# A softmax-attention and gated-FFN kernel on one core: down weights split one tile later, the last direct scores after the last product, two units in other blocks

## The chip, the cores and the metric

The kernel runs on one core of a Trainium2 chip. The metric is device time in microseconds (us). TensorE (PE) multiplies, VectorE (DVE) and ScalarE (ACT) work on tiles in SBUF and PSUM, GpSimd (POOL) does a little elementwise work and issues some DMAs, SyncE (SP) issues most DMAs. Each engine works through its own list of instructions in the order in which the program wrote them down, and semaphores hold it back where it needs another's result.

## The reference: what is computed

```python
xn = _layernorm(x)                         # x: 1 x 2048 x 512
s  = attention(xn, wqkv, wo)               # 32 heads of 16, softmax over all 2048 keys
g  = _silu((_silu(xn @ w_gate) * (xn @ w_up)) @ w_down)      # F = 1792
return x + s * g
```

Attention is `softmax(q k^T / 4) v` per head, then a product with `wo`. Everything is float32.

## The kernel before, in words

A prologue (about 165 us) normalises x, transposes it and makes q, k and v, which go to memory in DRAM. Then one main loop does attention and the FFN side by side on TensorE, and after it a short tail finishes the output.

**Attention in units and blocks.** A unit is one group of 4 heads (8 groups, `NG`) with 512 queries (4 of them, `NB`): 32 units, u0 to u31. Each goes over 16 key tiles of 128 keys. A unit is cut into blocks of 3 to 6 key tiles, by the planner at L460 to L478: units in `FINE` in four blocks of 4, unit 28 (`units - 4`) as 6, 6, 4, unit 0 as 4, 6, 6, unit 31 as 4, 3, 3, 3, 3, all others as two blocks of 5 and one of 6, the 6 where the FFN tile beside it is the largest. There are 101 blocks, numbered 0 to 100 in order of time.

**One block** is one call of `run(u, first, n)` (L856). It first does the scores of its n key tiles, mixed with products of the FFN, and then all its values (L916, `values`, matmul at L376: eight matmuls to a key tile). Each key tile has two score pairs (j = 0, 1), and each pair two halves. A pair takes one of two ways:
- *direct* (event `D`): two score matmuls at L872 into one of two double banks `score[0]`, `score[1]` in turn, then the exponential on ScalarE from there (L888, `pr<-score`). A direct score must wait until ScalarE is done with the score two before it.
- *copied* (events `A` and `B`): one matmul for each half into the one spare bank (`acc`), each moved out by VectorE (L900 and L906, `pr<-acc`), and at the end of the block one exponential in place (L912, `pr<-pr`). `B` must wait for the copy of `A`, the next `A` for the copy of `B`.

An `F` event is one step of the FFN: a pair of matmuls (`bankx`, `banky`, L186), taken from a generator by `fill` (L439). One FFN tile goes with one block.

**The order of events** is written by `events(n, f)` (L480) for n key tiles and f FFN steps: two direct scores at the start, the others spread with a gap of 4 to 5 places, the copies between them. In the list that it returns, the last event is always a product. `run` walks through the list.

**FFN tiles** come from `ffn(b)` (L195), b being 512 tokens. The 14 tiles of F are two groups of 7. For each group there are first seven *gate tiles* (gate and up products, f = 24 steps), each followed by tanh on ScalarE (L217) and two VectorE instructions (L218, L219) that give the hidden tile, and then four *down tiles* (21 steps each), evacuated by VectorE (L238 and L239, or L242 and L243 in the second group). After the last group of the last b comes a projection of the output for other tokens (`project_out`, two tiles of 9 steps and twelve of 12). With the second group's down tiles, `after` holds further work: `store_gate` (L188) and, for the last b, `next_out` (L261), which splits attention outputs and output weights for the projection.

**Splits.** A float32 operand is used as a high and a low part, so each gate-weight tile (`split_gu`, L130: three instructions), each hidden tile (`split_hidden`, L171: two) and each down-weight tile (`split_wd`, L151: a cast into `wd[:, f, 0]` and a subtraction into `wd[:, f, 1]`) is split on VectorE. These instructions are not written at once: they go into a list, `chores`, with a cost in steps. `run` takes chores from it (L908) when they fit in ahead of the next copy by its own reckoning, or freely when no copy is left; `tidy()` (L139) without an argument writes all of them at once. At the last event of a block (`final`, L876) and behind the block's events (L913) `tidy()` is called. `finish(u)` (L404) puts the closing work of a unit into the same list at the second direct score of the next unit: a transpose (L387), a reciprocal (L392), a scaling (L396) and, for every second group of heads, another transpose (L412).

**Loads.** `load_gu` (L121) and `load_wd` (L146) issue DMAs on SyncE. The raw down weights have one buffer (`wdr`), the raw gate weights two (`gur`). In `ffn`, a gate tile i loads the down weights of tile i and queues the gate split of tile i + 1 and the gate loads of tile i + 2 at its first step; the down-weight split of tile i is queued two steps before its end, so that it is written at the end of the same block.

Of the kernel before, what the change touches and what calls it, by code (L numbers as in the profile page):

```python
# [41 lines left out]
EARLY = 2  # L42
PROBS = 12
EPS = 1e-5
FINE = (27, 29, 30, 31)
QSLOT = (0, 1, 0)
KSLOT = (0, 0, 1)

# [2 lines left out]
def tile_block(ctx: ExitStack, tc: tile.TileContext, x, wqkv, wo, w_gate, w_up, w_down, out):  # L51
# [94 lines left out]
    def load_wd(i):  # L146
        raw = one.tile([P, D], F32, tag="wdr", name="wdr")
        sp.dma_start(raw, w_down[(i % NF) * P:(i % NF + 1) * P])
        wdr[i] = raw
# [45 lines left out]
    def ffn(b):  # L195
        for grp, part in enumerate(GROUPS):
            nf = part.stop - part.start
            for f in range(nf):
                i = b * NF + part.start + f
                if i:  # L200
                    load_wd(i)
                if i + 1 < NB * NF:
                    split_gu(i + 1)
                if i + 2 < NB * NF:
                    load_gu(i + 2)
                hi, lo = gu.pop(i)
                n = 0
                for c in range(DC):
                    for wt, j in ((hi, 0), (hi, 1), (lo, 0)):
                        both(wt[:, c], fx[:, j, c], n == 0, n == 3 * DC - 1)  # L210
                        n += 1
                        if n == 3 * DC - 2 and now > 0:
                            split_wd(f, i)
                        if n == 3 * DC:
                            th = one.tile([P, TB], F32, tag="th", name="th")
                            ga = two.tile([P, TB], F32, tag="ga", name="ga")
                            act(th, bankx, AF.Tanh, scale=0.5)  # L217
                            dve.scalar_tensor_tensor(ga, th, 1.0, bankx, op0=ALU.add, op1=ALU.mult)  # L218
                            dve.scalar_tensor_tensor(ga, ga, 0.5, banky, op0=ALU.mult, op1=ALU.mult)  # L219
                            kept.append((f, ga))  # L220
                            if now == 0:
                                split_wd(f, i)
                            if now >= 0:
                                split_hidden()
                            if grp == 1 and f == nf - 1 and b + 1 < NB:
                                load_fx(b + 1, 0)
                                load_fx(b + 1, 1)
                            elif grp == 1 and f == nf - 1:
                                load_wo(0)
                        yield 3 * DC - n  # L230
            for t in range(NT):
                n = 0
                for f in range(nf):
                    for a, w in ((0, 0), (0, 1), (1, 0)):
                        both(hh[:, f, a, t * P:(t + 1) * P], wd[:, f, w], n == 0, n == 3 * nf - 1)
                        n += 1
                        if n == 3 * nf and grp == 0:
                            dve.tensor_copy(facc[:, t], bankx)  # L238
                            dve.tensor_add(facc[:, t], banky, facc[:, t])  # L239
                        elif n == 3 * nf:  # L240
                            y = two.tile([P, D], F32, tag="ga", name="y")
                            dve.tensor_add(y, bankx, facc[:, t])  # L242
                            dve.tensor_add(y, banky, y)  # L243
                            after.append(partial(store_gate, y, b * TB + t * P))
                            if b == NB - 1:
                                after.append(partial(next_out, t))
                        yield 3 * nf - n
# [4 lines left out]
    def load_wo(c):  # L252
        wor[c] = one.tile([P, D], F32, tag="wdr", name="wor")
        sp.dma_start(wor[c], wo[c * P:(c + 1) * P])
# [206 lines left out]
    for u in range(units):  # L461
        opened.append(len(blocks))
        if u == units - 1:
            ns = [4, 3, 3, 3, 3]
        elif u == 0:
            ns = [4, 6, 6]
        elif u in FINE:
            ns = [4] * 4
        elif u == units - 4:
            ns = [6, 6, 4]  # L470
        else:
            ns = [5] * 3
            far = sizes[len(blocks):len(blocks) + 3]
            ns[far.index(max(far)) if far[1] < max(far) else 1] = 6
        kt = 0
        for n in ns:
            blocks.append((u, kt, n))
            kt += n  # L478

    def events(n, f):  # L480
        length = 2 * n + f
        need = 2 * n - max(2, (10 * length + 46) // 40)
        fit = 1 if ends and length < 24 else (10 * length + 34) // 112
        copied = max(0, min(need, fit)) if now else 0
        direct = 2 * n - copied
        gap = max(4, min(5, (length - 8) / max(1, direct - 2)))
        marks = [(0, "D"), (1, "D")] + [(7 + gap * i, "D") for i in range(direct - 2)]
        marks += [(2.2 + max(5.6, min(8, (length - 5) / (2 * copied))) * i, "AB"[i % 2]) for i in range(2 * copied)]
        marks.sort()
        out = []  # L490
        at = left = 0
        for t, kind in marks:
            while left < f - 1 and at < t:
                out.append((at, "F"))
                left += 1
                at += 1
            out.append((at, kind))
            at += 1 if kind == "D" else 0.5
        return direct, out + [(at + i, "F") for i in range(f - left)]
# [348 lines left out]
    on = [att.tile([P, TB], F32, name=f"on{b}") for b in range(NB)]  # L848

    now = 0  # L850
    split_hidden()
    split_wd(0, 0)
    tidy()
    ends = []

    def run(u, first, n):  # L856
        nonlocal lower
        g, b = divmod(u, NB)
        q = qst[u % 2]
        f = 0 if blocked() or not sizes else sizes.pop(0)  # L860
        direct, todo = events(n, f)
        if now == 0:
            for _ in range(4):
                todo.insert(0, todo.pop(max(i for i, (_, e) in enumerate(todo) if e == "F")))
        pairs = [(kt, j) for kt in range(first, first + n) for j in range(2)]
        straight, copies = pairs[:direct], pairs[direct:]
        probs, waiting = {}, []

        def scores(bank, kt, j, h):
            k, kc = kst[(g * NB + kt // CT) % RING], kt % CT  # L870
            r = slice(h * HALF, h * HALF + NROW)
            mm(bank, k[r, j, kc * P:(kc + 1) * P], q[r, j], start=True, stop=True)  # L872

        done = 0
        copying = [t + 1.5 for t, e in todo if e in "AB"]
        final = len(todo) - 1  # L876
        free = 0
        for at, (t, e) in enumerate(todo):
            if at == final:
                tidy()  # L880
            if e == "F":
                fill(1)
            elif e == "D":
                kt, j = straight[done]
                for h in order():
                    scores(score[done % 2][:, h], kt, j, h)
                probs[kt, j] = ppool.tile([P, 2, TB], F32, tag="pr", name="pr")
                act(probs[kt, j], score[done % 2], AF.Exp, scale=0.25)  # L888
                done += 1
                if done == 2:  # L890
                    while ends:
                        ends.pop(0)()
                    out_steps()
            elif e == "A":
                kt, j = copies.pop(0)
                waiting.append((kt, j))
                scores(spare_bank, kt, j, 0)
                lower = True
                probs[kt, j] = ppool.tile([P, 2, TB], F32, tag="pr", name="pr")
                dve.tensor_copy(probs[kt, j][:, 0], spare_bank)  # L900
                free = copying.pop(0) + 3
            else:
                kt, j = waiting[-1]
                scores(spare_bank, kt, j, 1)
                lower = False
                dve.tensor_copy(probs[kt, j][:, 1], spare_bank)  # L906
                free = copying.pop(0) + 3
            while chores and at < final and (not copying or max(free, t) + chores[0][0] <= copying[0] + 0.5):  # L908
                free = max(free, t) + chores[0][0]
                chores.pop(0)[1]()  # L910
        for kt, j in waiting:
            act(probs[kt, j], probs[kt, j], AF.Exp, scale=0.25)  # L912
        tidy()  # L913
        out_splits()
        catch_up()
        values(u, range(first, first + n), probs)  # L916
# [103 lines left out]
```

## Time and profile before

| | before |
|---|---|
| median of 3 runs | 1423.17 us (1421.42 to 1423.23) |
| the profiled execution | 1421.64 us |
| span of its instructions | 1419.9 us |
| granted TensorE clock | 1.000 |
| DMA moved | 148.17 MB, 104 GB/s on average |

The profile is of one execution; its span runs from the first to the last instruction. A line of a view names the line of the kernel (L376), the engine, the operation and `out<-in` by the names of the tiles. An idle time stands in brackets or behind a bar, with what ended it. The ends of matmuls are modelled, so two matmuls that look back to back can hide a short wait; the distance between starts is the safer reading.

### The profile page before, as it was taken

How to read it: one execution, taken by the hardware profiler on the slowest of the kernel's cores; microseconds unless marked ns; L12 is line 12 of the kernel's file. 1: busy time of each engine (PE TensorE's matmuls, PEld its weight loads, DVE VectorE, ACT ScalarE, POOL GpSimd, SP SyncE). 2: the span in 40 equal slices, each digit the busy share in tenths (PEclk: the TensorE clock that was granted, in tenths of full speed). 3: DMA queues.
4: the chain of work that ended last, by engine and by line, in shares of the span. 5: the costliest groups of instructions: out<-in, count | busy, mean ns of one | idle time of the engine just before them, and what ended most of it. 6: DMA issues, size and time to landing. Idle time of an engine off the chain costs nothing.

```text
span 1419.9 us, 27729 instructions
## 1 busy us (share of the span) xinstructions
PE 1403.0 (99%) x11227; PEld 847.5 (60%) x11227; DVE 756.3 (53%) x1279; ACT 1082.0 (76%) x1235; POOL 92.7 (7%) x104
## 2 busy tenths in 40 slices
PE   9999999999999999999999999999999999999998
PEld 7778665556555655565556555655565555564555
DVE  5543465355546553555455645554555355456556
ACT  5733587788788877787888787878787778687885
POOL 4200200000000000000000000000000000001333
PEclk9999999999999999999999999999999999999999
DMA  6768652043543421154514303365224112233333
GB/s 216 262 246 243 177 122 46 13 96 89 120 106 102 118 56 35 50 124 102 138 56 111 84 12 79 84 147 127 72 70 115 39 37 70 62 114 112 116 95 115
DMA packets 126956, 148.17 MB, mean 104 GB/s; under 512 B 12524, under 2 KB 79340, under 8 KB 126052
## 3 DMA queue, kind: packets, MB, share of 16 engines
q1 hardware_dynamic: 121620, 125.79, 34.7%
q0 software_dynamic: 4912, 20.12, 3.8%
q8 instruction: 91, 1.49, 0.4%
q14 instruction: 45, 0.37, 0.1%
q10 hardware_dynamic: 288, 0.39, 0.1%
HBM read 106.68 MB, written 39.58 MB: 103 GB/s over the span
## 4 chain that ended last, share of the span: by engine, by line
PE 94%; DVE 2%; ACT 2%; DMA 1%; issue 1%; SPq 0%; DVEq 0%; ACTq 0%
PE acc L376 30%; PE bankx L186 23%; PE score L872 16%; PE banky L186 10%; PE ps L626 6%; PE acc L872 3%; PE ps L628 3%; ACT pr L888 1%; DVE pr L900 0%; DMA v_d<-vt 0%; PE acc L601 0%; ACT pr L912 0%; DMA wraw<-in_A_wqkv_dram 0%; PE ps L657 0%; PE acc L957 0%
## 5 line engine op out<-in xcount | busy, mean ns | idle before, releaser
L888 ACT ACTIVATE pr<-score 128x1024 f32<-128x1024 f32 x862 | 812.0, 1033 | 244.5 <-PE score L872 243.2
L376 PE MATMUL acc<-pr,vst 128*17 128x512 f32 x4096 | 461.4, 593 | 0.0
L872 PE MATMUL score<-qst,kst 50*128 50x512 f32 x1724 | 396.1, 417 | 3.2 <-ACT pr L888 3.1
L186 PE MATMUL bankx<-fx,guh 64*128 64x512 f32 x896 | 331.5, 393 | 0.3 <-DVE ga L218 0.2
L186 PE MATMUL banky<-fx,guh 64*128 64x512 f32 x896 | 323.3, 393 | 0.3 <-DVE ga L219 0.3
L376 PEld LDWEIGHTS acc<-pr,vst 128*17 128x17 f32 x4096 | 111.3, 97 | 294.1 <-issue 284.0
L872 PEld LDWEIGHTS score<-qst,kst 50*128 50x128 f32 x1724 | 172.5, 184 | 158.6 <-issue 72.3
L900 DVE COPY pr<-acc 128x512 f32<-128x512 f32 x162 | 112.0, 691 | 171.6 <-PE acc L872 167.0
L186 PE MATMUL bankx<-wd,hh 64*128 64x512 f32 x672 | 200.2, 392 | 0.0
L186 PE MATMUL banky<-wd,hh 64*128 64x512 f32 x672 | 196.6, 391 | 0.0
L186 PEld LDWEIGHTS bankx<-fx,guh 64*128 64x128 f32 x896 | 166.4, 186 | 19.9 <-issue 0.9
L186 PE MATMUL banky<-fx,gul 64*128 64x512 f32 x448 | 175.3, 391 | 0.0
L186 PE MATMUL bankx<-fx,gul 64*128 64x512 f32 x448 | 175.3, 391 | 0.0
L186 PEld LDWEIGHTS banky<-fx,guh 64*128 64x128 f32 x896 | 166.3, 186 | 6.2 <-DVE ga L219 0.6
L912 ACT ACTIVATE pr<-pr 128x1024 f32<-128x1024 f32 x162 | 166.6, 1081 | 0.0
L906 DVE COPY pr<-acc 128x512 f32<-128x512 f32 x162 | 111.9, 691 | 88.4 <-PE acc L872 72.9
L872 PE MATMUL acc<-qst,kst 50*128 50x512 f32 x324 | 130.5, 403 | 5.2 <-issue 2.5
L186 PEld LDWEIGHTS bankx<-wd,hh 64*128 64x128 f32 x672 | 124.8, 186 | 13.1
L218 DVE SCALAR_TENSOR_TENSOR ga<-th,bankx 128x512 f32<-128x512 f32 x56 | 38.5, 687 | 166.3 <-ACT th L217 166.3
L186 PEld LDWEIGHTS banky<-wd,hh 64*128 64x128 f32 x672 | 124.9, 186 | 3.1
L186 PEld LDWEIGHTS bankx<-fx,gul 64*128 64x128 f32 x448 | 83.7, 187 | 9.9
L186 PEld LDWEIGHTS banky<-fx,gul 64*128 64x128 f32 x448 | 83.6, 186 | 2.6
(171 smaller groups left out, 1317.8 us busy)
## 6 DMA issues: line engine op xcount, KB each, us to landing
gur<-in_B_w_gate_dram SPq DMA_DIRECT2D x56, 256.0 KB
gur<-in_B_w_up_dram SPq DMA_DIRECT2D x56, 256.0 KB
wdr<-in_B_w_down_dram SPq DMA_DIRECT2D x56, 256.0 KB
kst<-k_d SPq DMA_DIRECT2D x192, 64.0 KB
qst<-q_d SPq DMA_DIRECT2D x192, 64.0 KB
fx<-xt_d SPq DMA_DIRECT2D x24, 512.0 KB
q_d<-parts SPq DMA_DIRECT2D x16, 512.0 KB
k_d<-parts SPq DMA_DIRECT2D x16, 512.0 KB
```

The source lines that it names most:

```text
L186: mm(banks[i], lhs[halves[i]], rhs[halves[i]], start=start, stop=stop)
L218: dve.scalar_tensor_tensor(ga, th, 1.0, bankx, op0=ALU.add, op1=ALU.mult)
L376: mm(acc[0][h * 32:h * 32 + DH + 1], v[:, kt % CT, h * (DH + 1):(h + 1) * (DH + 1)], probs[kt, h // 2][:, h % 2], start=kt == 0, stop=kt = ...
L626: mm(ps, w, a[:, c], start=n == 0, stop=n == 3 * DT - 1)
L628: mm(ps, a[:, c, tokens], w, start=n == 0, stop=n == 3 * DT - 1)
L872: mm(bank, k[r, j, kc * P:(kc + 1) * P], q[r, j], start=True, stop=True)
L888: act(probs[kt, j], score[done % 2], AF.Exp, scale=0.25)
L900: dve.tensor_copy(probs[kt, j][:, 0], spare_bank)
L906: dve.tensor_copy(probs[kt, j][:, 1], spare_bank)
L912: act(probs[kt, j], probs[kt, j], AF.Exp, scale=0.25)
```

## The change

Three things. The split of the down weights of a gate tile is queued in the next gate tile, behind that tile's gate split, and the load of the next down weights becomes a chore behind it; the split of a group's last down-weight tile is queued when the first down tile begins, and a `tidy()` stands behind it. (The hidden split of the very first tile, and its down-weight split, move from before block 0 into block 0.) `events` sorts a direct score up to 0.6 of a place ahead of a copy and lets a direct score follow the last product; `final` becomes the index of the last product. And unit 27 is cut like most units, unit 28 into 5, 4, 4, 3.

```diff
-FINE = (27, 29, 30, 31)
+FINE = (29, 30)
...
                 i = b * NF + part.start + f
-                if i:
-                    load_wd(i)
                 if i + 1 < NB * NF:
                     split_gu(i + 1)
+                if f:
+                    split_wd(f - 1, i - 1)
+                    chores.append((0, partial(load_wd, i)))
+                elif i:
+                    load_wd(i)
                 if i + 2 < NB * NF:
                     load_gu(i + 2)
...
                         n += 1
-                        if n == 3 * DC - 2 and now > 0:
-                            split_wd(f, i)
                         if n == 3 * DC:
...
                             kept.append((f, ga))
                             if now == 0:
-                                split_wd(f, i)
+                                kept.insert(0, first_hidden)
                             if now >= 0:
                                 split_hidden()
                             if grp == 1 and f == nf - 1 and b + 1 < NB:
                                 load_fx(b + 1, 0)
                                 load_fx(b + 1, 1)
-                            elif grp == 1 and f == nf - 1:
-                                load_wo(0)
                         yield 3 * DC - n
+            split_wd(nf - 1, b * NF + part.stop - 1)
+            if grp == 1 and b == NB - 1:
+                chores.append((0, partial(load_wo, 0)))
+            tidy()
             for t in range(NT):
...
         elif u == units - 4:
-            ns = [6, 6, 4]
+            ns = [5, 4, 4, 3]
...
-        marks.sort()
+        marks.sort(key=lambda mark: mark[0] - 0.6 * (mark[1] == "D"))
         out = []
         at = left = 0
         for t, kind in marks:
-            while left < f - 1 and at < t:
+            while left < f - (kind != "D") and at < t:
...
     now = 0
-    split_hidden()
-    split_wd(0, 0)
-    tidy()
+    first_hidden = kept.pop(0)
     ends = []
...
         copying = [t + 1.5 for t, e in todo if e in "AB"]
-        final = len(todo) - 1
+        final = max(at for at, (_, e) in enumerate(todo) if e == "F")
```

## The prediction

> **What bounds the kernel now.** The page first: how much of the span each engine is busy, and who is on the chain that ended last.
>
> ```profile
> span 1419.9 us, 27729 instructions
> PE 1403.0 (99%) x11227; PEld 847.5 (60%) x11227; DVE 756.3 (53%) x1279; ACT 1082.0 (76%) x1235; POOL 92.7 (7%) x104
> PE 94%; DVE 2%; ACT 2%; DMA 1%; issue 1%; SPq 0%; DVEq 0%; ACTq 0%
> ```
>
> TensorE carries 94% of the chain. The diff neither adds nor removes a matmul: each block keeps its rule for how many scores go direct and how many are copied, and the products and values are the same. So only the time in which TensorE waits between two matmuls can change, and I go through the blocks one kind at a time. The chain in order of time gives the length of each kind, because every block ends in a run of value matmuls (L376); the columns are start, length, what, count.
>
> ```profile
> 1127.31 4.42 PE acc L376 x40
> 1139.24 4.42 PE acc L376 x40
> ...
> 1166.03 4.42 PE acc L376 x40
> 1178.63 4.42 PE acc L376 x40
> 1191.93 5.28 PE acc L376 x48
> ...
> 1228.89 3.56 PE acc L376 x32
> 1239.41 3.56 PE acc L376 x32
> ```
>
> Eight value matmuls are one key tile. From these rows: a block of 5 key tiles with a down tile takes 1139.24 - 1127.31 = 11.93 us, one of 5 with a gate tile 1178.63 - 1166.03 = 12.60, one of 6 with a gate tile (1191.93 + 5.28) - (1178.63 + 4.42) = 14.16, one of 4 with a down tile 1239.41 - 1228.89 = 10.52.
>
> **The last direct score.** In a block of 6 key tiles with a gate tile, the list of events ends in direct score, two products, direct score, product; now the same last score comes after the last product, with three products between the two scores. There are 23 such blocks outside units 27 and 28. TensorE's timeline, first the end of one of them, then that of block 0, which already ends in three products and a score (four score or value matmuls are one row where they merge):
>
> ```profile
> 494.56 0.41 PE L872 MATMUL score<-qst,kst 50*128 50x512 f32 x2
> ...
> 495.37 0.50 PE L872 MATMUL score<-qst,kst 50*128 50x512 f32 x2
> ...
> 496.03 1.48 PE L376 MATMUL acc<-pr,vst 128*17 128x512 f32 x12
> ```
>
> ```profile
> 167.03 0.40 PE L872 MATMUL score<-qst,kst 50*128 50x512 f32 x2
> ...
> 167.96 0.40 PE L872 MATMUL score<-qst,kst 50*128 50x512 f32 x2
> ...
> 168.29 0.62 PE L376 MATMUL acc<-pr,vst 128*17 128x512 f32 x4
> ```
>
> Both stretches hold two scores and three products, and they take 496.03 - 494.56 = 1.47 us and 168.29 - 167.03 = 1.26. The difference, 0.21, is the score that came too early, waited for its bank and let the products behind it start alone. 23 x 0.21 = **-4.8 us** (bounds: 0, and 23 x 0.33 = -7.6, if the step from score to values went too). What hides the rest: the tanh of the tile now precedes the last exponential on ScalarE, and the values need the copied tile last.
>
> ```profile
> 487.69 9.46 ACT L888 ACTIVATE pr<-score 128x1024 f32<-128x1024 f32 x10 [2.73 <-PE score L872]
> ...
> 497.48 2.03 ACT L912 ACTIVATE pr<-pr 128x1024 f32<-128x1024 f32 x2
> ```
>
> ScalarE is through at 499.51, with the same instructions in either order; the sixth key tile is reached at 496.03 + 5 x 0.88 = 500.43, now at 500.22. The cover is 0.7 us.
>
> In the blocks of the output projection the same rule acts on blocks that ScalarE paces:
>
> ```profile
> 1287.88 0.50 PE L872 MATMUL score<-qst,kst 50*128 50x512 f32 x2 [0.41 <-ACT pr L888]
> 1288.54 3.63 PE L376 MATMUL acc<-pr,vst 128*17 128x512 f32 x32
> ```
>
> Here a score that waits 0.41 for an exponential is followed by one product and then the values. With the product ahead of the wait, the step score to values is 0.33 (block 0) instead of 0.66: three blocks (88, 92, 96), **-1.0 us** (0 to -2.0). Six blocks with two copied pairs end at ScalarE's last exponential instead:
>
> ```profile
> 1292.73 6.53 ACT L888 ACTIVATE pr<-score 128x1024 f32<-128x1024 f32 x7 [2.12 <-PE score L872]
> ...
> 1302.31 5.92 ACT L888 ACTIVATE pr<-score 128x1024 f32<-128x1024 f32 x6 [2.11 <-PE score L872]
> ```
>
> Seven in a row step by (6.53 - 1.03) / 6 = 0.92, so six need 5.6 and the 5.92 hold 0.3 of idling, because the second score of a copied tile stands three steps behind the first and waits for VectorE. Now it stands five steps behind and the last direct score ahead of it. I take 0.2 of the 0.3: 6 x 0.2 = **-1.2 us** (0 to -1.9). VectorE's evacuation of the bank moves ahead of the last copy; by my estimate the copy is then done 0.4 us before its exponential's turn. Five blocks of 6 key tiles with a down tile have a copy's second score one product later and so the next copy one step nearer: no row has this; a copy is 0.69 long and a step 0.23 (167.03 to 167.96 are four), so the margin moves by one step: **+0.4 us** (-0.3 to +1.0).
>
> **Units 27 and 28 in other blocks.** Before: 4, 4, 4, 4, 6, 6, 4 key tiles in blocks 81 to 87; now 5, 6, 5, 5, 4, 4, 3. Busy time of each engine in such blocks, and the sum over all seven:
>
> ```profile
> 1253.40:1267.90 14.50, 13.73 (x120) 8.21 (x116) 8.90 (x16) 12.03 (x13) 0.33 (x1) 1.00 0.20 66
> ...
> 1281.90:1292.10 10.20, 8.73 (x72) 4.03 (x68) 6.55 (x12) 7.57 (x8) 0.54 (x1) 1.00 0.17 54
> sum 82.20, PE 79.63 PEld 46.10 DVE 39.59 ACT 63.63 POOL 2.16; mean PE 11.38 PEld 6.59 DVE 5.66 ACT 9.09 POOL 0.31
> ```
>
> The first is a block of 6 with a down tile and three copied pairs, whose copies stand behind the gate and output-weight work that the tile before left on VectorE. Such tiles now fall into blocks of 4, which copy nothing. The new seven by kind: 12.60 + (14.16 - 0.21) + 11.93 + 11.93 + 10.52 + 10.52, and for 3 key tiles, from the blocks of 3 near the end,
>
> ```profile
> 1382.68 2.90 PE L376 MATMUL acc<-pr,vst 128*17 128x512 f32 x24
> 1389.95 2.90 PE L376 MATMUL acc<-pr,vst 128*17 128x512 f32 x24
> ```
>
> 7.27 and 0.2 for its first copy, which still stands behind that work: 7.5. Sum 78.9 against 82.20: **-3.3 us** (-1.5, if blocks 84 and 87 each wait 0.9 more for a copy, to -4.5).
>
> **Down weights one tile later.** Inside a gate tile, the two instructions that split a down-weight tile move from VectorE's idle time before the gate to VectorE's idle time between copies; TensorE has no wait on them at either place, so 0. The load of the next tile, formerly the first thing that SyncE issued for a tile, is now queued behind the gate loads and waits there for the split. Behind it on SyncE stand the attention loads that the end of the block issues, whose buffers come free only then: 0, as long as the split comes before the end of the block, some 6 us later. The load of the output weights moves one tile back and still has a whole block of 11.93 us before its use. But the split of the seventh tile of a group is queued at the first down product, and a full flush stands right behind it: everything queued for VectorE is issued there, ahead of the first score copy of that block. In three of the eight such blocks (6, 39, 72) a unit begins too, and its closing work is in the queue. VectorE in block 39, and TensorE's second half of that copy:
>
> ```profile
> 670.29 0.69 DVE L900 COPY pr<-acc 128x512 f32<-128x512 f32 x1
> 670.90 0.41 DVE L396 TENSOR_TENSOR on<-o,rl 128x256 f32<-128x256 f32 x1
> ...
> 672.37 0.70 DVE L412 STREAM_TRANSPOSE o<-on 128x512 f32<-128x512 f32 x1
> ```
>
> ```profile
> 671.33 0.39 PE L872 MATMUL acc<-qst,kst 50*128 50x512 f32 x1
> ```
>
> ```profile
> L910 DVE CAST wd<-wdr x55: 415/419/429, 174.1 to 1224.5; 128x512 fp32r<-128x512 f32 x55
> L910 DVE TENSOR_TENSOR wd<-wdr,wd x55: 691/693/694, 174.6 to 1225.0; 128x512 fp32r<-128x512 f32 x55
> ```
>
> The copy at 670.29 ends at 670.98, 0.35 before the score at 671.33 that overwrites its bank. Now 0.41 (L396), 0.70 (L412), 0.42 and 0.69 (the split) come first: 2.2 us later, 1.9 late. Block 72 is the same; block 6 (an even group of heads) has no L412: 1.5 later, 1.1 late. Nothing gives this back, as TensorE is the bound: 1.9 + 1.9 + 1.1 = **+4.9 us**. In the other five blocks only the 1.1 us of split is issued, with VectorE idle before it: 0. Bounds: 0, and 4.9 + 5 x 1.1 = +10.4.
>
> That an instruction of VectorE is not passed by a later one is seen at the start of the main loop:
>
> ```profile
> 177.22 0.69 DVE L910 CAST guh<-gur 128x1024 fp32r<-128x1024 f32 x1 [0.86 <-DMA gur<-in_B_w_up_dram]
> 177.83 0.68 DVE L900 COPY pr<-acc 128x512 f32<-128x512 f32 x1
> ```
>
> ```profile
> 178.61 0.46 PE L872 MATMUL acc<-qst,kst 50*128 50x512 f32 x1 [2.47 <-issue]
> ```
>
> ```profile
> 170.82 0.43 SPq L148 DMA_DIRECT2D wdr<-in_B_w_down_dram  x1
> ```
>
> The gate cast waited for its load, the copy behind it waited too, and TensorE stood 2.47 us for the copy. [...]
>
> At this same place the down-weight load (0.43 of SyncE's issue) moves behind the gate loads, so the cast may start that much earlier: **-0.5 us** (-1.0 to 0). The wait of VectorE for the attention pool's memory (hidden split of tile 0) now lies behind a gate split, which only clears the first gate product; that gain ends in the same wait for the load.
>
> **Sum.** -4.8 - 1.0 - 1.2 + 0.4 - 3.3 + 4.9 - 0.5 = -5.5 us. Against the profiled execution's own 1421.64 us (its span is 1419.9) this is 1416.1. The median of the runs shown is 1423.17, 1.5 above that execution; I forecast the median: **1417.7 us**.
>
> **Rivals.**
>
> *The flush is free* (chance 0.18). The 4.9 falls away: -10.4, 1412.8 us. For it: VectorE is 53% busy. Against it: the two rows at 670.29 and 671.33 leave 0.35 us for 2.2.
>
> *The score moves, the time does not* (0.12). ScalarE gives the moved score back at the end of the values: without the terms 4.8, 1.0 and 1.2 the sum is +1.5, 1424.7 us. For it: ScalarE has 12.03 of 14.50 us in the window above. Against it: the cover of 0.7 us worked out above.
>
> *The down weights come late* (0.13), on the slower side. A tile's load is now issued only after the split of the tile before; if it has not landed at the flush, VectorE waits there with the copy behind it. VectorE has waited for these loads:
>
> ```profile
> DVE wd L910 <- DMA wdr<-in_B_w_down_dram: 13.4, 7, 3.4
> ```
>
> ```profile
> 943.22 0.38 SPq L148 DMA_DIRECT2D wdr<-in_B_w_down_dram  x1
> ```
>
> ```profile
> 947.65 0.43 DVE L910 CAST wd<-wdr 128x512 fp32r<-128x512 f32 x1 [1.00 <-DMA wdr<-in_B_w_down_dram]
> ```
>
> Seven waits of 1.9 on average; at all eight flushes that is +15.3, the sum +9.8, 1433.0 us. It decides from 5.5 / 8 = 0.7 us a flush. Against it: the load above took 4.4 us from issue to use, and there are some 6 from the middle of a block to the flush.
>
> **Chances and range.** Forecast 0.57, its own range 1414 to 1421. A measurement of this kernel can tell about 0.2% (2.8 us) from no change, so "same" is 1420.3 to 1426.0. Faster: 0.54 of the forecast and 0.18, 0.72. Same: 0.03 of the forecast and 0.12, 0.15. Slower: 0.13. The range takes in the first two rivals with the bounds of the small terms and leaves the third out: 1411.5 to 1425.0.
>
> **What would show it.** Blocks of 6 with a gate tile end in score, then values, and take 13.95 instead of 14.16. Near 243, 669 and 1094 us VectorE has four (three) more instructions ahead of L900, and TensorE a wait of 1 to 2 us for the copy. Blocks 81 to 87 take about 79 us. No wait of a down-weight split for its load. I am wrong if those three waits are missing, if any of the other five flushes shows one, or if value matmuls wait for exponentials in the gate blocks.

## The result, and the profile after

| | before | after |
|---|---|---|
| median | 1422.93 us (6 runs, 1421.42 to 1424.28) | 1417.66 us (6 runs, 1415.51 to 1419.65) |
| ratio | | 0.9965, 95% interval 0.9952 to 0.9977 |
| profiled execution | 1421.64 us, span 1419.9 | 1417.50 us, span 1415.7 |

The kernel became 0.35% faster; 1417.7 us were forecast. The page of the changed kernel has the same matmuls and the same balance:

```profile
span 1415.7 us, 27730 instructions
PE 1399.6 (99%) x11227; PEld 853.3 (60%) x11227; DVE 756.9 (53%) x1281; ACT 1081.4 (76%) x1235; POOL 92.0 (7%) x104
PE 86%; DVE 1%; ACT 1%; issue 0%; DVEq 0%; ACTq 0%
```

The last line is the chain of work that ended last. Its 86% can't be laid beside the 94% of before: this time the view follows the chain back only to 160 us, the start of the main loop, so its shares sum to 88%. As before, everything is decided by how long TensorE waits between two matmuls, and the page can't say where. For that I cut the main loop of both traces into its 101 blocks, each from the start of its first score to the start of the next block's first score in TensorE's timeline, and sum the lengths by kind (us; the last column is after minus before):

| blocks | number | before | after | difference |
|---|---|---|---|---|
| 6 key tiles, gate tile (without block 1) | 22 | 312.02 | 307.24 | -4.78 |
| 81 to 87 (units 27 and 28) | 7 | 82.25 | 78.96 | -3.29 |
| output blocks with two copied pairs | 6 | 57.32 | 55.60 | -1.72 |
| output blocks 88, 92, 96 | 3 | 28.80 | 28.37 | -0.43 |
| 6 key tiles, down tile | 5 | 67.09 | 68.19 | +1.10 |
| 6, 39, 72: flush and unit begin together | 3 | 35.82 | 40.74 | +4.93 |
| block 1 | 1 | 18.32 | 18.74 | +0.42 |
| all others | 54 | | | 0.05 |

These add up to -3.7; the main loop also begins 0.4 us earlier. Together that is the 4.1 to 4.2 us between the two profiled executions. The medians lie 5.3 apart; runs of one kernel differ by 3 to 4 us, so the remaining 1.1 us belong to no block.

**The moved score.** The end of a gate block of 6 key tiles in TensorE's timeline, to be laid beside 494.56 to 496.03 of before:

```profile
495.14 0.40 PE L873 MATMUL score<-qst,kst 50*128 50x512 f32 x2
496.09 0.40 PE L873 MATMUL score<-qst,kst 50*128 50x512 f32 x2
496.42 0.62 PE L379 MATMUL acc<-pr,vst 128*17 128x512 f32 x4
```

Score, three products, score, values: 1.28 us, where it was 1.47. The same in an output block paced by ScalarE (block 92):

```profile
1332.95 0.51 PE L873 MATMUL score<-qst,kst 50*128 50x512 f32 x2 [0.41 <-ACT pr L889]
1333.39 1.48 PE L379 MATMUL acc<-pr,vst 128*17 128x512 f32 x12
```

The score still waits 0.41 for an exponential, but the values follow after 0.44 instead of 0.66.

**Units 27 and 28.** Busy time of the engines in the last of the seven blocks, and the sum over all seven:

```profile
1282.62:1290.09 7.47, 7.47 (x58) 3.72 (x54) 6.31 (x11) 5.76 (x6) 0.32 (x1) 1.00 0.25 66
sum 78.96, PE 78.96 PEld 45.84 DVE 42.11 ACT 63.42 POOL 2.16; mean PE 11.28 PEld 6.55 DVE 6.02 ACT 9.06 POOL 0.31
```

Before, TensorE was busy in 79.63 of 82.20 us; now it has no gap in the view at all.

**The flush.** VectorE at the start of block 39, and the waits of TensorE over the whole span (who, for whom, total, times, longest):

```profile
669.58 0.43 DVE L399 TENSOR_TENSOR on<-o,rl 128x256 f32<-128x256 f32 x1
670.04 0.71 DVE L415 STREAM_TRANSPOSE o<-on 128x512 f32<-128x512 f32 x1
670.67 0.38 DVE L142 CAST wd<-wdr 128x512 fp32r<-128x512 f32 x1
671.09 0.69 DVE L142 TENSOR_TENSOR wd<-wdr,wd 128x512 fp32r<-128x512 f32 x1
671.70 0.68 DVE L901 COPY pr<-acc 128x512 f32<-128x512 f32 x1
```

```profile
PE acc L873 <- DVE pr L901: 3.8, 3, 1.5
PE acc L873 <- issue: 2.9, 1, 2.9
```

Four instructions stand ahead of the copy that used to be the first, and TensorE waits for that copy three times. The view counts 3.8 us; the blocks are 4.9 longer. In block 39 it counts 1.51, but the first start behind the wait comes 1.90 us after the last one ahead of it (670.54 to 672.44), and the next 0.34 later (672.78), where the steps after that are 0.22 to 0.24. The fourth wait, 2.9 us, is that of block 1.

### The profile page after: what moved, and what is told of

It is laid out like the page before. It is cut to its first block, busy times and chain, and to the rows that moved or that the text cites. A ratio compares the mean times of both kernels' runs of the same rounds, so it can differ in the third digit from the quotient of the medians.

```text
span 1415.7 us, 27730 instructions
## 1 busy us (share of the span) xinstructions
PE 1399.6 (99%) x11227; PEld 853.3 (60%) x11227; DVE 756.9 (53%) x1281; ACT 1081.4 (76%) x1235; POOL 92.0 (7%) x104
## 4 chain that ended last, share of the span: by engine, by line
PE 86%; DVE 1%; ACT 1%; issue 0%; DVEq 0%; ACTq 0%
PE acc L379 32%; PE bankx L186 24%; PE score L873 16%; PE banky L186 11%; PE acc L873 3%; ACT pr L889 1%; PE acc L958 0%; DVE wd L142 0%; PE banky L958 0%; DVE o L390 0%; DVE pr L901 0%; PE score L958 0%; DVE o L415 0%; DVE on L399 0%; DVE rl L395 0%
```

## The experiments

Times are medians; before was run beside each.

### The flush taken away

```diff
                             if now >= 0:
                                 split_hidden()
+                            if f == nf - 1:
+                                split_wd(f, i)
+                                if grp == 1 and b == NB - 1:
+                                    chores.append((0, partial(load_wo, 0)))
...
-            split_wd(nf - 1, b * NF + part.stop - 1)
-            if grp == 1 and b == NB - 1:
-                chores.append((0, partial(load_wo, 0)))
-            tidy()
```

> The changed kernel with one part undone: the split of a group's seventh down-weight tile is queued behind that tile's hidden split, in the last gate tile, and nothing is flushed at the first down product. If the flush is what costs 4.9 us (blocks 6, 39 and 72 at 13.1, 13.8, 13.8 us instead of 12.0, 11.9, 11.9), those three blocks come back to 12.0 to 12.3 and the kernel takes about 4.2 us less than the changed one, 8 to 9 us less than before. If these blocks are long for another reason (the loads that run at that time, the clock), they stay at 13 to 14 us and the time is that of the changed kernel.

Measured: 1412.65 us (5 runs), 0.9933 of before, 0.9919 to 0.9946, and 5.0 us less than the changed kernel. Blocks 6, 39 and 72 sum to 35.79, against 35.82 before and 40.74 in the changed kernel; no other kind of block moves by more than 0.1, block 1 (18.28) apart. VectorE around the start of block 39 of this kernel:

```profile
666.92 0.42 DVE L142 CAST wd<-wdr 128x512 fp32r<-128x512 f32 x1
667.38 0.69 DVE L142 TENSOR_TENSOR wd<-wdr,wd 128x512 fp32r<-128x512 f32 x1
...
668.90 0.63 DVE L901 COPY pr<-acc 128x512 f32<-128x512 f32 x1
669.45 0.41 DVE L399 TENSOR_TENSOR on<-o,rl 128x256 f32<-128x256 f32 x1
```

The same split lies in the values of the block before, where VectorE has nothing to do, and the copy comes first again. The 4.9 us were the flush with the split in it, and a wait of VectorE for the load, which the third rival feared, doesn't appear even 3 us earlier.

### Each part alone

The kernel before with one part of the diff each: the new order of events with the new `final`, the new blocks of units 27 and 28, the later down-weight split with its flush.

> The kernel before with the new order of events alone. If the score that moves behind the last product saves by itself, the blocks of 6 key tiles with a gate tile take 13.96 instead of 14.16 us (23 of them: -4.6), the output blocks lose 0.2 each (about -1.5), and the blocks of 6 with a down tile gain 0.2 each (7 of them: +1.4): about -4.7 us against before. If the saving needs the down-weight split out of the way at the end of the tile, those blocks stay at 14.1 to 14.2 us and the time is within 1 us of before.

Measured: 1415.52 us, 0.9957 of before (0.9944 to 0.9971). The 22 gate blocks sum to 307.25, as in the whole change; output blocks -1.77 and -0.72, down blocks +1.08. The 7.1 us are more than expected: output blocks with two copied pairs gave 0.3 each, not 0.2, block 1 came out 0.5 shorter, and the main loop began 0.4 us earlier.

> The kernel before with units 27 and 28 alone in other blocks. If the gain comes from down tiles that meet no score copies, blocks 81 to 87 sum to about 79.2 us instead of 82.2 and the kernel takes 3.0 us less. If it needs the new order of events in the seven blocks, the sum stays above 81 us and the gain is under 1 us.

Measured: 1418.08 us, 0.9975 of before (0.9966 to 0.9984). Blocks 81 to 87 sum to 79.55, 2.70 less than before. Block 1 was 0.6 shorter (17.70), though this edit doesn't touch it: so much it differs between two executions of the same instructions. The medians say -4.5, the profiled executions -3.7; what goes beyond the 2.7 us is not the edit's as far as the blocks show.

> The kernel before with the later down-weight split alone (and with it the flush). If the parts add up, the three blocks 6, 39 and 72 cost 4.9 us, block 1 about 0.4 more, nothing else moves, and the kernel is 5 us slower than before. If the later split frees time in the gate blocks that the other two parts then use, the gate blocks get shorter here and the kernel is less than 3 us slower.

Measured: 1428.65 us, 1.0040 of before (1.0027 to 1.0054). The three flush blocks cost 6.5, block 1 0.8, and the gate blocks don't move (312.12). The parts add up, -7.1, -4.5 and +6.1 us to -5.5 where the change as a whole measured -5.3, but with intervals of 1.3 to 1.9 us on each part the closeness is chance; the sums by blocks are the better evidence. That the later split frees anything for the gate blocks is refuted: they take 307.25 us without it and 307.24 with it. The 1.6 us over the expected 4.9 sit in block 39 alone. TensorE's wait there, and the engines' busy time and granted clock (the 1.00 or 0.50 ahead of the last two columns) in two windows of 3.41 us:

```profile
675.34 0.49 PE L873 MATMUL acc<-qst,kst 50*128 50x512 f32 x1 [1.51 <-DVE pr L901]
```

```profile
672.97:676.38 3.41, 1.90 (x15) 1.31 (x14) 2.79 (x5) 1.76 (x2) 0.54 (x1) 1.00 1.08 207
676.38:679.79 3.41, 3.41 (x18) 2.67 (x16) 0.88 (x2) 2.17 (x3) 0.00 (x0) 0.50 1.06 207
```

The wait is the same 1.5 us as in the changed kernel (the longest in its view of waits above). But behind it TensorE's granted clock was 0.50 for 3.41 us, and its view has 18 matmuls in that time, against 33 in the 3.41 us behind it at 1.00.

### Block 1

The forecast had block 1 0.5 us shorter, and it was 0.4 longer. VectorE in block 1 of the changed kernel, then busy time and clock in four windows of the changed kernel and two of before:

```profile
175.84 0.69 DVE L911 CAST guh<-gur 128x1024 fp32r<-128x1024 f32 x1 [3.37 <-DMA gur<-in_B_w_up_dram]
176.45 0.68 DVE L901 COPY pr<-acc 128x512 f32<-128x512 f32 x1
```

```profile
170.26:173.59 3.33, 3.33 (x30) 1.94 (x24) 2.15 (x4) 1.56 (x2) 2.30 (x2) 1.00 0.75 179
173.59:177.00 3.41, 0.71 (x7) 0.24 (x3) 1.16 (x2) 1.30 (x2) 0.00 (x0) 1.00 1.11 231
177.00:180.42 3.42, 3.18 (x16) 2.75 (x18) 2.36 (x5) 1.21 (x2) 0.00 (x0) 0.50 0.82 183
180.42:183.83 3.41, 3.41 (x32) 3.06 (x30) 1.98 (x3) 3.29 (x4) 0.00 (x0) 1.00 0.30 54
```

```profile
173.87:177.28 3.41, 2.24 (x16) 1.56 (x15) 2.21 (x5) 1.51 (x2) 0.00 (x0) 1.00 0.98 196
177.28:180.70 3.42, 2.09 (x18) 2.00 (x20) 3.12 (x5) 1.29 (x2) 0.00 (x0) 1.00 1.02 227
```

The load did come earlier: the cast starts 4.4 us after the block's first score (175.84 - 171.46), before it was 5.4 (177.22 - 171.85). But the first products no longer wait for their banks, so TensorE reaches the missing copy earlier and waits longer in one piece (2.94 us, before 2.47). Then the clock falls to 0.50 for 3.42 us. Before, TensorE was busy for 2.24 and 2.09 us of the two windows in which it waited, and the clock stayed at 1.00. From 170 to 192 us the mean granted clock is 0.92 in the changed kernel, without the flush and with the later split alone, which all have the later split and splits ahead of the copies, and 1.00 with the new order alone and with units 27 and 28 alone, which have the old place of the split. The length of the block is less sure: 18.32 and 17.70 us in two traces with the instructions of before, 18.74, 18.28 and 18.24 in three with those of the changed kernel. The next experiment takes the wait away: in block 1, no split is written ahead of a copy.

```diff
-            while chores and at < final and (not copying or ...):
+            while chores and at < final and not (now == 1 and copying) and (not copying or ...):
```

> The changed kernel, but in block 1 no queued split is written ahead of a score copy (all of them come after the last copy). If TensorE's stop in block 1 is the first copy standing behind a gate cast that waits for its load, the block takes 14.0 instead of 18.7 us, no stretch of it runs at half the granted clock, and the kernel takes 4.8 us less than the changed one. If the start is bound by the loads themselves (attention keys, gate weights), the wait comes back in block 1 or 2 at another instruction, and the gain stays under 1.5 us.

Measured: 1412.96 us, 0.9926 of before (0.9913 to 0.9939), 4.7 less than the changed kernel. Block 1 takes 13.94 us. Busy time and clock over 20 us of its start:

```profile
170.00:190.00 20.00, 20.00 (x176) 12.12 (x170) 14.06 (x24) 15.80 (x18) 2.56 (x3) 1.00 0.73 167
```

No gap, no slow clock, and no later wait in their place: the gate cast needed its data only for the next block.

### The sorting in the down tiles

```diff
-        marks.sort(key=lambda mark: mark[0] - 0.6 * (mark[1] == "D"))
+        marks.sort(key=lambda mark: mark[0] - 0.6 * (mark[1] == "D" and f != 3 * FG))
```

> The changed kernel without the new sorting of direct scores before copies in the down tiles (it stays in the others). If the five blocks of 6 key tiles with a down tile lost 0.2 us each by it, they are back at 13.3 to 13.5 us, and the kernel takes 1.1 us less than the changed one, which is at the edge of what can be measured. If the loss came from the last direct score or from the down weights, they stay at 13.5 to 13.7.

Measured: 1416.97 us, 0.9958 of before (0.9944 to 0.9971); by the time alone this can't be told from the changed kernel. The five blocks sum to 67.34 instead of 68.19, 0.84 of the 1.10. Two score copies in one of them (block 52), before, after, and here:

```profile
839.76 0.46 PE L872 MATMUL acc<-qst,kst 50*128 50x512 f32 x1
...
841.09 0.41 PE L872 MATMUL acc<-qst,kst 50*128 50x512 f32 x1
```

```profile
840.77 0.39 PE L873 MATMUL acc<-qst,kst 50*128 50x512 f32 x1
...
841.94 0.49 PE L873 MATMUL acc<-qst,kst 50*128 50x512 f32 x1
```

```profile
839.60 0.47 PE L873 MATMUL acc<-qst,kst 50*128 50x512 f32 x1
...
840.92 0.42 PE L873 MATMUL acc<-qst,kst 50*128 50x512 f32 x1
```

With one step less between them the second waits for its bank: 1.17 us is what score and copy take (the copy between them runs from 841.19 to 841.88). Before there were 1.33 us, and here there are 1.32 again.

### All three together

> The changed kernel with all three: no flush at the first down product, no split ahead of a copy in block 1, the old sorting in the down tiles. If the costs are separate, 4.9 + 4.8 + 1.1 = 10.8 us less than the changed kernel, about 1407 us. If taking one wait away only uncovers the next, clearly less than 8 us.

Measured: 1407.30 us (4 runs, 1407.06 to 1407.42), 0.9886 of before (0.9869 to 0.9903), 10.4 less than the changed kernel. The costs are separate, and this version beats both.

### Waits of chosen length

To see whether the wait alone halves the clock, idle additions were put on VectorE ahead of the first copy of nine blocks in the middle of the loop.

> The kernel with all three, and in nine blocks of 5 key tiles with a down tile (8, 20, 29, 31, 41, 53, 62, 64, 74) one clearing and 3, 4, 5, 6, 3, 4, 5, 6 and 8 additions of an idle tile on VectorE ahead of the first score copy, which the output does not use. TensorE then waits some 1.9 to 5 us in the middle of the loop. If it was the wait that halved the granted clock in block 1 of the changed kernel, the longer of these pauses are followed by a few us at half the clock, and each such block is longer by its pause and 1.5 to 2 us more. If it was something of the start (loads at full DMA load), the clock stays at 1.00 and each block is longer by its pause alone.

Measured: 1416.57 us (one run). The additions depended on nothing and ran ahead while VectorE was free, so TensorE waited only 1.3 to 2.7 us, and its mean granted clock over the span was 1.00. As a test of the clock it was inconclusive, so the pauses were tied to the score:

```diff
-                    dve.memset(idle, 0.0)
+                    dve.tensor_copy(idle, spare_bank)
```

> As the nine pauses before, which ran ahead in VectorE's idle time and so made TensorE wait only 1.3 to 2.7 us. Here each begins with a copy of the score bank, so that it can't start before the score: a copy and 2, 2, 3, 3, 4, 4, 5, 5 and 7 additions, waits of about 1.6, 2.2, 2.8, 3.4 and 4.7 us. If a wait alone halves the granted clock, at least the waits of 2.8 us and over are followed by 3.4 us at 0.5 and 1.5 to 2 us of extra time in their blocks, and whether the shorter ones are depends on where they fall in windows of 3.4 us. If the start and block 39 had another cause, the clock stays at 1.00 in all nine blocks.

Measured: 1448.21 us (one run), with a mean granted clock of 0.988 over the span. Six of the nine waits are followed by half the clock for 3.41 or 6.83 us; the two of 1.4 us are not, and one of the two of 2.9 us is not. These last two, in blocks 41 and 53, have the same four additions and the same wait; TensorE's row and the windows around each:

```profile
706.60 0.79 PE L874 MATMUL acc<-qst,kst 50*128 50x512 f32 x1 [2.87 <-DVE pr L907]
...
864.89 0.50 PE L874 MATMUL acc<-qst,kst 50*128 50x512 f32 x1 [2.87 <-DVE pr L907]
```

```profile
702.95:706.36 3.41, 0.77 (x7) 0.33 (x4) 3.27 (x6) 1.65 (x2) 0.00 (x0) 1.00 0.04 13
706.36:709.77 3.41, 3.17 (x16) 2.52 (x18) 0.87 (x2) 1.02 (x1) 0.00 (x0) 0.50 0.00 0
```

```profile
859.96:863.37 3.41, 2.06 (x17) 1.43 (x13) 2.62 (x4) 2.88 (x3) 0.00 (x0) 1.00 0.00 0
863.37:866.79 3.42, 1.90 (x16) 1.60 (x18) 2.13 (x4) 0.83 (x1) 0.00 (x0) 1.00 0.00 0
```

Block 41 became 4.7 us longer, block 53 3.3. Of the first wait (703.73 to 706.60) 2.63 us lie in one of these windows of 3.41 us, of the second (862.02 to 864.89) 1.35 and 1.52 in two. DMA is all but at rest in all four (0.04 at most), so the loads of the start are not needed for a drop.

## Why the prediction was right, point by point

- **Moved score, gate blocks**: forecast -4.8 for 23 blocks, measured -4.78 for the 22 besides block 1, 0.3 of it a chance wait that block 37 had before. The order alone gives it.
- **Output blocks with two copied pairs**: forecast -1.2, measured -1.72. In block 90 two waits for VectorE, 0.52 us together, also went away.
- **Blocks 88, 92, 96**: forecast -1.0, measured -0.43. The step from the score to the values is 0.44, not the 0.33 of block 0, and block 88 gained nothing. With the new order alone it takes 9.36 us, with the shorter block 87 ahead of it 9.63, as before (9.61). Its first copy starts 1.24 to 1.25 us after the block's first score in all three. But in the changed kernel ScalarE starts its first exponential 0.91 us after that score (1291.00 - 1290.09), with the new order alone 0.63 (1288.17 - 1287.54), and the scores that wait for ScalarE come as much later. Why that exponential starts late isn't shown.
- **Down blocks of 6**: forecast +0.4 with bounds -0.3 to +1.0, measured +1.10, outside. The step was right (the second score nearer to the next copy), and its size was not: the margin was 0.15 us (1.32 against 1.17), and in block 52 the next products start 0.33 us behind the late score (841.94 to 842.27), where the steps after that are 0.23 to 0.24.
- **Units 27 and 28**: forecast 78.9 us, measured 78.96.
- **Flush**: forecast +4.9 in blocks 6, 39 and 72 and 0 in the other five, measured +4.93 and 0.06 for the four of these outside unit 27. The first rival (the flush is free) is refuted by these blocks, and by the kernel without the flush.
- **Block 1**: forecast -0.5, measured +0.42 in one execution each, where the block differs by 0.6 between executions. The step "the cast may start that much earlier" held, by 1.0 us; what failed is that the earlier cast would shorten the block; the sum also took a wait to cost its length alone. TensorE was busy for 0.71 of the 3.41 us from 173.59, and behind them came 3.42 us at a granted clock of 0.50.
- **The rivals on time**: that ScalarE takes the moved score back is refuted, as the blocks kept the whole 0.2 us. The late down weights didn't come: VectorE has no wait for that load in the changed kernel.

The gate blocks, units 27 and 28 and the flush came out as worked out, and they carry the direction and most of the size. The closeness of -5.3 to -5.5 is luck. By the blocks of the two profiled executions the terms that missed are off by -0.5, +0.6, +0.7 and +0.9 us, the sum is -3.7 and not -5.5, the earlier start of the main loop, which was not forecast, takes 0.4, and the last 1.1 us come from the spread of the runs.

## What to carry to other kernels

When one engine is the bound and its work does not change, cut the trace into the stages of the loop and price each kind by the distance between starts; the busy share of the page is 99% for the kernels of 1423 and 1407 us alike, and the view of waits counted 3.8 us where the blocks grew by 4.9. A list of deferred work that is flushed at once puts all of it ahead of whatever is written next: look for the instruction that the bound waits for, and put the flush behind it. And a wait of the bound can cost more than its length: of two equal waits of 2.87 us the one with half the clock behind it (block 41) made its block 4.7 us longer, the other (block 53) 3.3.

## What the runs showed of the hardware

TensorE's granted clock fell from 1.00 to 0.50 behind windows of 3.41 us in which TensorE was busy for 0.71 us (from 173.59, the changed kernel), 0.77 and 1.62 (from 702.95 and 539.11, the tied pauses) and 1.90 (from 672.97, the down-weight split alone). It stayed at 1.00 behind windows of the same length with 1.90, 1.98 and 2.06 us busy (from 863.37, 266.04 and 859.96, the tied pauses) and with 2.09 and 2.24 (from 177.28 and 173.87, before):

```profile
266.04:269.45 3.41, 1.98 (x17) 1.37 (x15) 2.75 (x5) 2.00 (x3) 0.00 (x0) 1.00 0.00 0
```

This is busy time with modelled ends. Of the two windows with 1.90 us busy one lost the clock and one kept it; what decided between them isn't shown.

The clock was at 0.50 for 3.42 us in the changed kernel (177.00 to 180.42) and for 3.41 with the down-weight split alone (676.38 to 679.79). With the tied pauses it was so for 3.41 us from 706.36 and for 6.83, twice as long, from 542.52, with TensorE busy for 3.05 and 3.42 us of the two halves. These last two drops are 163.84 us apart, 48 times 3.413; the border at 863.37, which divides the wait of block 53, is 46 times 3.413 behind 706.36. That the place of a wait between such borders decides was not tried by itself.

With the same pause and the same wait, block 41, with a drop, became 4.69 us longer and block 53, without one, 3.33.
